# Three experts' weights behind the gather, float64 blocks on ScalarE's queue, routing begun earlier

## The chip, the core and the metric

The kernel runs on one core of a Trainium2 chip. The metric is device time in microseconds (us), the median over several executions. TensorE does the matrix products, VectorE and ScalarE the element work, GpSimd some element work and the indirect DMAs; SyncE issues most other DMAs. Operands live in SBUF, products land in PSUM.

## The reference, cut to what matters

Three stages, each feeding the next.

```python
# attention: q, k, v (2, 8, 768, 64): window of 16 keys beside block summaries
x = attn_out.transpose(0, 2, 1, 3).reshape(1536, 512)
# mixture of 8 experts, each takes 192 tokens, in the order of the gate's logits
logits = x @ w_gate
order = np.argsort(-logits.flatten())
for idx in order:                      # greedy: best logit first
    tok, e = idx // 8, idx % 8
    if assigned[tok] >= 0 or counts[e] >= 192: continue
    assigned[tok] = e; counts[e] += 1
for e in range(8):
    out[assigned == e] = relu(x[assigned == e] @ w1[e]) @ w2[e]
# solu layer: w_in (512, 1024), w_out (1024, 512), both float64
h = x @ w_in
solu = h * softmax(h)
result = (layernorm(solu) * g_ln) @ w_out
```

w_in and w_out are float64 arrays; the kernel loads their two 32-bit words as integers and builds a high and a low float32r part from them.

## The kernel before, in words

**Attention** (to about 103 us) runs over 24 units of four query tiles, with TensorE's and SyncE's order written out by hand in a plan. Its last outputs x are stored to the DRAM tile xd. In it, w_in's first three blocks of float64 are loaded (`load64`, line 58) and split (`split64`, line 63).

**A split** of a block of 128x512 is: ScalarE's Abs with a scale (line 70), three integer steps on VectorE (lines 72, 74, 75), ScalarE's copy to the high part (line 77), and the low part as a difference, on GpSimd in two halves of 256 (line 79). There are 16 blocks, eight of w_in (wiH, wiL) and eight of w_out (woH, woL). Splits carry a priority of -3000, so the planner puts their instructions behind others that are ready; `after` and `late` name an instruction behind which a split is issued.

**Routing.** `route(n)` finds the next expert that fills up and its 192 tokens, without a sort: five levels of a search over the digits of the logits' keys. A level is a comparison on VectorE (`compare`, line 124, tile ge), twelve small products on TensorE (line 502), a step on VectorE (line 507) and one product with ones (lines 510, 516). Then come a chain of small VectorE steps, three products that give positions (lines 548 to 550), two comparisons ohs with their twelve index products each (lines 558 to 563), the index tiles, and `gather`, two indirect DMAs from GpSimd that fetch the token rows xg from xd. As soon as the expert's number is known (line 530), SyncE loads the first three of its eight weight chunks (512 KB each). `route` is a generator: before each of its TensorE steps it yields a time, from the table HOPS, for which TensorE is to be given other work.

**Experts.** Expert n has 32 pieces of four products 128x192 in float32: 16 for w1 (`hidden`, whose result ScalarE copies into hT) and 16 for w2 (`result`, into yh and yl). All eight experts take this path (WHOLE is 7). Products go to one of two PSUM tiles, m1. `tokens(n)` transposes the gathered rows and ScalarE copies them into xs, of which there is one buffer.

**Solu layer.** Tokens leave the experts in tiles of 128, twelve of them. For tile k, `solu_in` is eight pieces of three products 128x512, then the softmax and the norm on VectorE and ScalarE, `solu_t` eight transposes, `solu_out` eight pieces, and an indirect DMA to the output.

**The order of the expert phases.** TensorE's order is the program's. In phase n the 32 pieces of expert n are woven with the solu work of tiles that are ready (`stage2`), and the steps of `route(n + 1)` and `tokens(n + 1)` are put in where the time that they asked for has been filled by pieces. The other engines' orders come from the planner.

**The float64 blocks after the attention.** `todo` lists the 13 blocks left, `steps` the place of each: after a given expert, kind (h or r) and piece group. Two are split with the first routing, the rest in the phases of the first two experts. Loads go through SyncE's queue, three ahead, each waiting for one of three raw buffers.

Of the kernel before, what the change touches and what calls it, by code (L numbers as in the profile page):

```python
# [8 lines left out]
F32 = mybir.dt.float32  # L9
F32R = mybir.dt.float32r  # L10
BF = mybir.dt.bfloat16
I32 = mybir.dt.int32
# [9 lines left out]
def tile_attention_moe_solu(ctx, tc, q, k, v, w_gate, w1, w2, w_in, w_out, g_ln, out):  # L22
# [32 lines left out]
    wiL = keep.tile([128, KD, FF], F32R, name="wiL")  # L55


    def load64(cv, src, n, bufs):
        raw = cv.tile([128, n, 2], I32, name="raw", bufs=bufs)
        dma(raw.rearrange("p n t -> p (n t)"), src.bitcast(I32))  # L60
        return raw

    def split64(cv, raw, hi, lo, after=None, late=None):
        n = hi.shape[1]
        with tc.high_priority(-3000):
            y = cv.tile([128, n], F32, name="cy")
            h = cv.tile([128, n], I32, name="ch", bufs=2)

            with tc.issue_after(after.ins) if after is not None else nullcontext():
                nc.scalar.activation(y, raw[:, :, 1].bitcast(F32), AF.Abs, scale=2.0 ** -112)  # L70
            with tc.issue_after(late.ins) if late is not None else nullcontext():
                nc.vector.tensor_scalar(h, y.bitcast(I32), 3, 0x3FFFFFF8, op0=OP.logical_shift_left,
                                        op1=OP.bitwise_and)
            nc.vector.scalar_tensor_tensor(h, raw[:, :, 1], -0x40000000, h, op0=OP.bitwise_and, op1=OP.bitwise_or)
            nc.vector.scalar_tensor_tensor(h, raw[:, :, 0], 29, h, op0=OP.logical_shift_right, op1=OP.bitwise_or)
            h = h.bitcast(F32)
            nc.scalar.copy(hi, h)
            for c in range(0, n, 256):
                nc.gpsimd.tensor_tensor(lo[:, c:c + 256], h[:, c:c + 256], hi[:, c:c + 256].bitcast(F32), op=OP.subtract)


    ones = keep.tile([128, 128], BF, name="ones")
# [38 lines left out]
    def compare(out, x, a, b, op):  # L121

        n = x.shape[1]
        nc.vector.tensor_tensor(out, x.rearrange("p (j t) -> p j t", t=2)[:, :, None, :].to_broadcast(  # L124
            [128, n // 2, b - a, 2]), ios[:, None, a:b, :].to_broadcast([128, n // 2, b - a, 2]), op=op)
# [305 lines left out]
    NCA = 3  # L431
    RAW64 = {}

    def load_in(cv, i, bufs):
        kk, hf = divmod(i, 2)
        RAW64[i] = load64(cv, w_in[128 * kk:128 * kk + 128, 512 * hf:512 * hf + 512], 512, bufs)

    def split_in(cv, i, *after):
        kk, hf = divmod(i, 2)
# [8 lines left out]
    with tc.manual_schedule(engines={mybir.EngineType.PE, mybir.EngineType.SP}):  # L448
# [3 lines left out]
        for u in sorted(plan):  # L452
# [8 lines left out]
    pm = ctx.enter_context(tc.tile_pool(name="pm", bufs=1, space=PSUM))  # L461


    HOPS = [(1600, 1760, 560, 2200, 2320, 5600),
            (1750, 1540, 490, 2450, 2030, 6300),
            (2620, 2200, 700, 4000, 2900, 8520),
            (2500, 2200, 700, 4500, 2900, 9000),
            (2500, 2200, 700, 2900, 2900, 27000)]
# [4 lines left out]
    def route(ph):  # L473
# [84 lines left out]

        for i, (lo, hi) in enumerate(((0, 128), (128, CAP))):
            compare(ohs[:, :, lo:hi], slot, lo, hi, OP.is_equal)  # L560
            for j in range(NJ):
                nc.tensor.matmul(pi[:, 2 * i:2 * i + 2], ohs[:, j // 2, hi - 128:hi, j % 2], info[:, j, :],
                                 start=j == 0, stop=j == NJ - 1)
# [16 lines left out]
            LI = index(oidx[t0 + 1], 0, 128, 64)  # L580
            IDX[ph] = [(oidx[t0], 128), (oidx[t0 + 1], 64)]
        gather(ph)
        if ph == 0:

            e2 = rp.tile([1, 1], I32, name="e2")
            with tc.issue_after(GI[-1].ins):
                nc.gpsimd.tensor_copy(e2, ei[0:1])
            EREG[ph] = nc.sync.value_load(e2, min_val=0, max_val=E - 1)
            load_w(ph, 3, NCK)
        elif ph <= WHOLE:  # L590
            load_w(ph, 3, NCK)
# [64 lines left out]
    def tokens(ph):  # L656

        o = 0
        if ph > WHOLE:
            xs = mp.tile([128, KD, 2, CAP], F32R, name="xs")  # L660
        else:
            xs = mp.tile([128, 2 * KD, CAP], F32, name="xs")[:, :KD]
        for x, n in XG.pop(ph):
            p = pm.tile([128, 4, 128], F32, name="tr", bufs=2)
            for d in range(KD):
                nc.tensor.transpose(p[:, d, 0:n], x[0:n, 128 * d:128 * d + 128], ident[0:n, 0:n])  # L666
            if ph > WHOLE:
                nc.scalar.copy(xs[:, :, 0, o:o + n], p[:, :, 0:n])
                nc.vector.tensor_tensor(xs[:, :, 1, o:o + n], p[:, :, 0:n], xs[:, :, 0, o:o + n].bitcast(F32),
                                        op=OP.subtract)  # L670
            else:
                nc.scalar.copy(xs[:, :, o:o + n], p[:, :, 0:n])  # L672
            o += n
        XS[ph] = xs
# [27 lines left out]

    def hidden(ph, f, part):
        if f == part == 0:
            HT[ph] = mp.tile([128, KF, 2, CAP], F32R, name="hT") if ph > WHOLE else mp.tile([128, 2 * KF, CAP], F32, name="hT")
        h = HT[ph]
        p = product(ph, W[ph][f // 2], 128 * (f % 2), KD, XS[ph], part)
        if p is None:
            return
        if ph <= WHOLE:  # L710
            after(ph, "h", f, nc.scalar.activation(h[:, f], p[:, :CAP], AF.Relu))  # L711
            return
        s = mp.tile([128, CAP], F32, name="hs", bufs=3)
        nc.scalar.copy(s, p[:, CAP:])
        nc.vector.tensor_tensor(s, s, p[:, :CAP], op=OP.add)
        a = nc.scalar.activation(h[:, f, 0], s, AF.Relu)
        nc.vector.scalar_tensor_tensor(h[:, f, 1], s, 0.0, h[:, f, 0].bitcast(F32), op0=OP.max, op1=OP.subtract)
        after(ph, "h", f, a)
# [103 lines left out]

    nc.vector.memset(mhalf, -0.5)
    ctx.enter_context(tc.manual_schedule(engines={mybir.EngineType.PE}))
    for _ in route(0):
        pass
    dma(gb, g_ln.partition_broadcast(128))
    cvb = tc.tile_pool(name="cvb", bufs=1)
    cvp = cvb.__enter__()

    NRAW = 3
    todo = [(load_in, split_in, i) for i in range(NCA, 2 * KD)]

    def load_out(cv, i, bufs):
        RAW64[8 + i] = load64(cv, w_out[128 * i:128 * i + 128], DM, bufs)

    def split_out(cv, i, after):
        split64(cv, RAW64.pop(8 + i), woH[:, i], woL[:, i], after)

    todo += [(load_out, split_out, i) for i in range(KI)]  # L840
    steps = [None, None, (0, "h", 2), (0, "h", 4), (0, "h", 6), (0, "r", 1), (1, "h", 0), (1, "h", 2), (1, "h", 3),
             (1, "h", 5), (1, "h", 7), (1, "r", 1), (1, "r", 2)]

    def step64(n, *after):
        todo[n][1](cvp, todo[n][2], *after)
        if n + NRAW < len(todo):
            todo[n + NRAW][0](cvp, todo[n + NRAW][2], NRAW)

    for n in range(NRAW):
        todo[n][0](cvp, todo[n][2], NRAW)  # L850
    for n, st in enumerate(steps):
        if st is None:
            step64(n, None, LAST[0])
        else:
            HOOK.setdefault(st, []).append((step64, n))

    p = pm.tile([128, DM], F32, name="o", bufs=1)
    for i in range(40):
        nc.tensor.matmul(p[:, 0:128], ones, tri, start=True, stop=True)
    early = route(1)  # L860
    for _ in range(3):
        next(early)
    tokens(0)
    def weave(a, b):

# [23 lines left out]


    stage2 = ["", "i0", "i1 o0 i2", "o1 i3 o2", "i4 o3 i5", "o4 i6 o5", "i7 o6 i8", "o7 i9 o8", "i10 o9 i11 o10 o11"]
    for ph in range(E):
        u = 540 if ph > WHOLE else 650
        g1 = [(u, hidden, ph, f, i) for f in range(KF) for i in range(KD // 2)]
        g2 = [(u, result, ph, d, i) for d in range(KD) for i in range(KF // 2)]
        other = []
        for k, l in items(stage2[ph]):
            assert k <= last(ph - 1)
            other += l
        if ph == 1:  # L900

            other.append((1300, lambda: None))
        work = weave(g1 + g2, other)

        def ahead(n):
            yield from early if n == 1 else route(n)
            yield HOPS[0 if n <= 1 else 1 if n == 2 else 4 if n == E - 1 else 2 + n % 2][5]
            tokens(n)

        hops = ahead(ph + 1) if ph + 1 < E else iter(())  # L910
        wait = next(hops, None)
        for cost, f, *a in work:
            while wait is not None and wait < cost / 2:
                wait = next(hops, None)
            f(*a)
            if wait is not None:
                wait -= cost
        for _ in hops:
            pass

        if ph == 1:
            cvb.__exit__(None, None, None)
            ml = ctx.enter_context(tc.tile_pool(name="ml", bufs=1))
    for _, l in items(stage2[E]):
        for _, f, *a in l:
            f(*a)
# [30 lines left out]
```

## Time and profile before

| | |
|---|---|
| time, median of 3 runs | 497.45 us (496.35 to 497.51) |
| the profiled execution | 498.66 us |
| its span, first to last instruction | 497.0 us |
| mean granted TensorE clock | 0.968 of full speed |
| TensorE busy | 447.6 us (90%) |
| VectorE busy | 274.3 us (55%) |
| ScalarE busy | 176.0 us (35%) |
| GpSimd busy | 89.0 us (18%) |
| moved by DMA | 64.61 MB, mean 130 GB/s |

Busy times are unions over the span of one execution. PE is TensorE's products, PEld its weight loads, which overlap them; DVE is VectorE, ACT ScalarE, POOL GpSimd, SPq SyncE's queue of DMA issues. The granted clock is the share of full speed that TensorE was given: 1.00 is 2.4 GHz, 0.50 is 1.2 GHz.

### The profile page before, as it was taken

How to read it: one execution, taken by the hardware profiler on the slowest of the kernel's cores; microseconds unless marked ns; L12 is line 12 of the kernel's file. 1: busy time of each engine (PE TensorE's matmuls, PEld its weight loads, DVE VectorE, ACT ScalarE, POOL GpSimd, SP SyncE). 2: the span in 40 equal slices, each digit the busy share in tenths (PEclk: the TensorE clock that was granted, in tenths of full speed). 3: DMA queues.
4: the chain of work that ended last, by engine and by line, in shares of the span. 5: the costliest groups of instructions: out<-in, count | busy, mean ns of one | idle time of the engine just before them, and what ended most of it. 6: DMA issues, size and time to landing. Idle time of an engine off the chain costs nothing.

```text
span 497.0 us, 9767 instructions
## 1 busy us (share of the span) xinstructions
PE 447.6 (90%) x3723; PEld 387.7 (78%) x3723; DVE 274.3 (55%) x1033; ACT 176.0 (35%) x425; POOL 89.0 (18%) x150
## 2 busy tenths in 40 slices
PE   2799999845778988999999999999999999999995
PEld 1668688634678868789888988988898899998773
DVE  7658577878594697675256526626662322213441
ACT  3578778711233432331321413123141313222331
POOL 9311200302324243202000200200020110100012
PEclk9999999975798998999999999999999999999999
DMA  9979861363869159008304800740390560000001
GB/s 195 195 158 207 220 181 40 109 231 131 272 218 368 54 180 316 1 2 279 113 1 137 257 21 1 243 149 1 118 275 30 179 205 1 1 22 1 22 21 42
DMA packets 92463, 64.61 MB, mean 130 GB/s; under 512 B 25728, under 2 KB 87168, under 8 KB 92416
## 3 DMA queue, kind: packets, MB, share of 16 engines
q1 hardware_dynamic: 90432, 57.70, 41.2%
q0 software_dynamic: 1984, 6.29, 3.5%
q8 instruction: 29, 0.48, 0.4%
q14 instruction: 18, 0.15, 0.1%
HBM read 56.51 MB, written 6.29 MB: 126 GB/s over the span
## 4 chain that ended last, share of the span: by engine, by line
PE 71%; DVE 12%; DMA 6%; ACT 5%; issue 3%; SPq 1%; POOL 0%; POOLq 0%; DVEq 0%; ACTq 0%
PE m L694 28%; PE h L759 13%; PE o L802 11%; PE pS L332 4%; PE pO L361 2%; DVE ge L124 2%; DMA xg<-xd,oidx 2%; PE pr L502 2%; PE pA L348 1%; DVE ex L768 1%; DMA wl<-in_moe_w_dram 1%; DMA kn<-in_k_dram 1%; PE tr L666 1%; ACT s L341 1%; PE T L255 1%
## 5 line engine op out<-in xcount | busy, mean ns | idle before, releaser
L694 PE MATMUL m<-xs,wr 128*128 128x192 f32 x384 | 79.7, 341 | 1.2 <-ACT xs L672 1.1
L694 PEld LDWEIGHTS m<-xs,wr 128*128 128x128 f32 x384 | 65.2, 195 | 6.2 <-ACT xs L672 1.4
L742 DVE TENSOR_TENSOR yl<-m,yh 128x128 fp32r<-128x128 f32 (+1 forms) x64 | 16.2, 253 | 82.1 <-ACT yh L741 82.1
L711 ACT ACTIVATE hT<-m 128x192 f32<-128x192 f32 x64 | 21.2, 331 | 90.0 <-PE m L694 76.6
L694 PE MATMUL m<-hT,wh 128*128 128x192 f32 x256 | 51.7, 332 | 0.0
L694 PE MATMUL m<-hT,wl 128*128 128x192 f32 x256 | 50.7, 335 | 0.0
L694 PEld LDWEIGHTS m<-hT,wl 128*128 128x128 f32 x256 | 45.0, 195 | 3.3
L694 PEld LDWEIGHTS m<-hT,wh 128*128 128x128 f32 x256 | 44.5, 193 | 3.7
L741 ACT CAST yh<-m 128x128 fp32r<-128x128 f32 (+1 forms) x64 | 15.2, 238 | 88.9 <-PE m L694 80.6
L341 ACT ACTIVATE s<-s,mx 128x120 f32<-128x120 f32 x96 | 31.5, 387 | 13.6 <-DVE mx L338 13.4
L759 PE MATMUL h<-wiH,yh 128*128 128x512 f32 x96 | 34.4, 446 | 0.0
L332 PE MATMUL pS<-kTw,qbd 128*128 128x120 f32 x192 | 27.8, 290 | 5.8 <-DVE kTw L315 4.8
L777 POOL TENSOR_TENSOR st<-st,mhalf 128x1 f32<-128x1 f32 x12 | 6.9, 574 | 144.8 <-DVE st L776 104.8
L759 PE MATMUL h<-wiL,yh 128*128 128x512 f32 x96 | 32.3, 424 | 0.0
L759 PE MATMUL h<-wiH,yl 128*128 128x512 f32 x96 | 32.2, 424 | 0.0
L802 PE MATMUL o<-woH,lh 128*128 128x512 f32 x96 | 30.8, 432 | 1.3 <-ACT lh L791 1.3
L802 PE MATMUL o<-woL,lh 128*128 128x512 f32 x96 | 32.0, 429 | 0.0
L332 PEld LDWEIGHTS pS<-kTw,qbd 128*128 128x128 f32 x192 | 24.8, 202 | 7.6 <-issue 6.0
L124 DVE TENSOR_TENSOR ge<-e,ios 128x1536 bf16<-128x1536 bf16 (+3 forms) x37 | 29.7, 803 | 0.8
L802 PE MATMUL o<-woH,ll 128*128 128x512 f32 x96 | 29.4, 418 | 0.0
L764 DVE TENSOR_REDUCE st<-h 128x1 f32<-128x1024 f32 x12 | 14.7, 1224 | 26.4 <-PE h L759 26.4
L338 DVE CUSTOM_DVE_ANT_0 s<-pS,mask 128x120 f32<-128x120 f32 x96 | 21.4, 278 | 12.4 <-PE pS L332 5.5
(184 smaller groups left out, 823.5 us busy)
## 6 DMA issues: line engine op xcount, KB each, us to landing
wr<-in_moe_w_dram SPq DMA_DIRECT2D x24, 512.0 KB
wl<-in_moe_w_dram SPq DMA_DIRECT2D x20, 512.0 KB
wh<-in_moe_w_dram SPq DMA_DIRECT2D x20, 512.0 KB
raw<-in_moe_w_in_dram SPq DMA_DIRECT2D x8, 512.0 KB
raw<-in_moe_w_out_dram SPq DMA_DIRECT2D x8, 512.0 KB
Vw<-in_v_dram SPq DMA_DIRECT2D x20, 192.0 KB
kn<-in_k_dram SPq DMA_DIRECT2D x8, 384.0 KB
qn<-in_q_dram SPq DMA_DIRECT2D x8, 384.0 KB
```

Of the source, the lines that this page charges most:

```text
L124: nc.vector.tensor_tensor(out, x.rearrange("p (j t) -> p j t", t=2)[:, :, None, :].to_broadcast([128, n // 2, b - a, 2]), ios[:, None, a:b ...
L332: nc.tensor.matmul(p[:, n, :], qbd[i][:, t, :], kTw[i][:, t, :], start=True, stop=True)
L338: nc.vector.tensor_tensor_reduce(s[:, n, :], p[:, n, :], m, scale=1.0, scalar=3.0e38, op0=OP.add, op1=OP.min, accum_out=mx[:, n:n + 1])
L341: EXPS[u] = nc.scalar.activation(s[:, n, :], s[:, n, :], AF.Exp, bias=mx[:, n:n + 1], scale=-1.0)
L361: nc.tensor.matmul(p[o:o + 64, n // 2, h, :], a[:, n, 64 * h:64 * h + 64], Vw[:, b, t, 2 * hp + h, :], start=True, stop=True)
L694: nc.tensor.matmul(p[:, :CAP], w[:, d, o:o + 128], rhs[:, d], start=d == 0, stop=d == n - 1)
L711: after(ph, "h", f, nc.scalar.activation(h[:, f], p[:, :CAP], AF.Relu))
L741: a = nc.scalar.copy(hi, s[:, s0:s0 + n])
L742: nc.vector.tensor_tensor(YL[k][:, d, c:c + n], s[:, s0:s0 + n], hi.bitcast(F32), op=OP.subtract)
L759: nc.tensor.matmul(ps, a[:, d, :], w[:, d, 512 * s:512 * s + 512], start=n == 0, stop=n == len(mm) - 1)
L764: nc.vector.tensor_reduce(st[:, 0:1], p, axis=AX.X, op=OP.max)
L802: nc.tensor.matmul(p, a[:, f, :], w[:, f, :], start=n == 0, stop=n == len(mm) - 1)
```

## The change

- `load64` can be issued by another engine; the loads of all blocks after the attention but the first two come from ScalarE's queue, the load of block n + 2 at the place of block n's split, ahead of it.
- The low part in `split64` is one subtraction of 512 on VectorE. This holds for all 16 blocks, those in the attention too.
- The blocks' places: five blocks of w_in in the first expert's phase, in the order 4, 6, 3, 5, 7; w_out's eight in the second's (six) and the third's (two). None is split with the first routing any more.
- For the first three routings, not only the first, chunks 3 to 7 of the expert's weights are loaded after the expert's number has been copied by GpSimd behind the gather.
- HOPS: longer times for the first three routings. From the second on there is a yield of 650 between the two ohs comparisons' index products.
- Filler products of 128x128 in bf16, results unused: 18 in each of the last two waits of the first routing, and 90 between the first seven steps of the second routing, which now all stand ahead of the first tokens; before, three steps did, behind 40 fillers.
- The generator of the routings runs on over the phases: after the second expert's tokens, up to five steps of the third routing are put into the first phase.
- xs and hT are half as large (the other half was unused), and the pools cvb and ml are open side by side.

```diff
-    def load64(cv, src, n, bufs):
+    def load64(cv, src, n, bufs, eng=None):
         raw = cv.tile([128, n, 2], I32, name="raw", bufs=bufs)
-        dma(raw.rearrange("p n t -> p (n t)"), src.bitcast(I32))
+        (eng or nc.sync).dma_start(raw.rearrange("p n t -> p (n t)"), src.bitcast(I32))
...
             nc.scalar.copy(hi, h)
-            for c in range(0, n, 256):
-                nc.gpsimd.tensor_tensor(lo[:, c:c + 256], h[:, c:c + 256], hi[:, c:c + 256].bitcast(F32), op=OP.subtract)
+            nc.vector.tensor_tensor(lo, h, hi.bitcast(F32), op=OP.subtract)
...
-    HOPS = [(1600, 1760, 560, 2200, 2320, 5600),
-            (1750, 1540, 490, 2450, 2030, 6300),
+    HOPS = [(1900, 1760, 560, 2300, 2600, 6300),
+            (1900, 1760, 560, 2600, 2600, 7000),
...
             compare(ohs[:, :, lo:hi], slot, lo, hi, OP.is_equal)
+            if i and ph:
+                yield 650
...
-        if ph == 0:
+        if ph < 3:
 
             e2 = rp.tile([1, 1], I32, name="e2")
...
-            xs = mp.tile([128, 2 * KD, CAP], F32, name="xs")[:, :KD]
+            xs = mp.tile([128, KD, CAP], F32, name="xs")
...
-    for _ in route(0):
-        pass
+    idle = pm.tile([128, DM], F32, name="o", bufs=1)
+
+    def fill(n):
+        for _ in range(n):
+            nc.tensor.matmul(idle[:, 0:128], ones, tri, start=True, stop=True)
+
+    for wait in route(0):
+        fill(18 if wait > 2000 else 0)
...
-    todo = [(load_in, split_in, i) for i in range(NCA, 2 * KD)]
+    todo = [(load_in, split_in, i) for i in (4, 6, 3, 5, 7)]
...
-    steps = [None, None, (0, "h", 2), (0, "h", 4), (0, "h", 6), (0, "r", 1), (1, "h", 0), (1, "h", 2), (1, "h", 3),
-             (1, "h", 5), (1, "h", 7), (1, "r", 1), (1, "r", 2)]
+    steps = [(0, "h", 1), (0, "h", 3), (0, "h", 5), (0, "r", 1), (0, "r", 2), (1, "h", 1), (1, "h", 4), (1, "h", 6),
+             (1, "r", 1), (1, "r", 2), (1, "r", 3), (2, "h", 0), (2, "h", 1)]
 
     def step64(n, *after):
+        if n + NRAW - 1 < len(todo):
+            todo[n + NRAW - 1][0](cvp, todo[n + NRAW - 1][2], NRAW, nc.scalar)
         todo[n][1](cvp, todo[n][2], *after)
-        if n + NRAW < len(todo):
-            todo[n + NRAW][0](cvp, todo[n + NRAW][2], NRAW)
...
-    p = pm.tile([128, DM], F32, name="o", bufs=1)
-    for i in range(40):
-        nc.tensor.matmul(p[:, 0:128], ones, tri, start=True, stop=True)
     early = route(1)
-    for _ in range(3):
+    for n in (12, 6, 20, 6, 20, 6, 20):
         next(early)
+        fill(n)
     tokens(0)
...
+    READY = set()
+
+    def ahead():
+        for n in range(1, E):
+            yield from early if n == 1 else route(n)
+            yield HOPS[0 if n <= 1 else 1 if n == 2 else 4 if n == E - 1 else 2 + n % 2][5]
+            tokens(n)
+            READY.add(n)
+            yield 0
+
+    hops = ahead()
+    wait, extra = next(hops), 5
...
             while wait is not None and wait < cost / 2:
+                if ph + 1 in READY:
+                    if ph or extra == 0:
+                        wait = None
+                        break
+                    extra -= 1
                 wait = next(hops, None)
```

## Rows read from the trace of the kernel before

**Rows 1.** Stretches: length; PE, PEld, DVE, ACT, POOL busy; clock, DMA share, GB/s.
```profile
128.80:162.70 33.90, 29.26 (x204) 27.23 (x205) 19.68 (x70) 9.52 (x24) 8.71 (x10) 0.87 0.91 299
162.70:201.80 39.10, 34.21 (x254) 29.73 (x253) 31.20 (x92) 15.30 (x36) 13.20 (x14) 0.96 0.54 172
201.80:476.60 274.80, 272.73 (x1789) 240.77 (x1790) 121.26 (x426) 71.80 (x179) 27.68 (x33) 1.00 0.30 94
```

**Rows 2.** TensorE in order of time: start, duration, line, count, idle before.
```profile
118.55 0.95 PE L562 MATMUL pr<-info,ohs 128*128 128x2 bf16 x24 [1.94 <-DVE ohs L124]
119.36 4.43 PE L859 MATMUL o<-tri,ones 128*128 128x128 bf16 x40
...
127.66 0.69 PE L666 MATMUL tr<-ident,xg 64*128 64x64 f32 x4 [0.18 <-DMA xg<-xd,oidx]
...
148.10 6.10 PE L694 MATMUL m<-hT,wl 128*128 128x192 f32 x36
...
156.60 0.66 PE L666 MATMUL tr<-ident,xg 128*128 128x128 f32 x4 [0.83 <-DMA xg<-xd,oidx]
157.09 5.75 PE L694 MATMUL m<-hT,wl 128*128 128x192 f32 x24
```

**Rows 3.** TensorE's waits, first and second phase: total us, times, longest.
```profile
PE tr L666 <- DMA xg<-xd,ix: 1.1, 1, 1.1
...
PE tr L666 <- DMA xg<-xd,oidx: 0.8, 1, 0.8
...
PE m L694 <- ACT xs L672: 1.1, 1, 1.1
```

**Rows 4.** TensorE by microsecond: length, busy, then clock, DMA share, GB/s.
```profile
106.00:107.00 1.00, 0.00 (x0) 0.80 0.72 238
...
133.00:134.00 1.00, 1.00 (x15) 0.55 1.15 348
```

**Rows 5.** VectorE in order of time.
```profile
106.11 0.96 DVE L124 TENSOR_TENSOR ge<-e,ios 128x1536 bf16<-128x1536 bf16 x1
106.99 0.16 DVE L506 SCALAR_TENSOR_TENSOR eb<-e,d5b 128x12 f32<-128x12 bf16 x1
...
108.28 0.96 DVE L124 TENSOR_TENSOR ge<-e,ios 128x1536 bf16<-128x1536 bf16 x1
...
117.54 1.43 DVE L124 TENSOR_TENSOR ohs<-slot,ios 128x1536 bf16<-128x1536 bf16 x2
...
125.70 2.89 DVE L506 SCALAR_TENSOR_TENSOR eb<-e,d5b 128x12 f32<-128x12 bf16 x1
...
141.05 0.71 DVE L525 TENSOR_SCALAR ine<-r,r 128x12 f32<-128x12 f32 x1
...
145.27 2.46 DVE L124 TENSOR_TENSOR ohs<-slot,ios 128x1536 bf16<-128x1536 bf16 x2
...
188.05 0.78 DVE L606 SCALAR_TENSOR_TENSOR wt<-slot,wt 128x96 f32<-128x96 bf16 x1
```

**Rows 6.** GpSimd in order of time.
```profile
120.74 3.57 POOL L649 DMA_INDIRECT xg<-xd,oidx  x1 [22.24 <-DVE ch L72]
...
125.80 2.76 POOL L79 TENSOR_TENSOR wiL<-ch,wiH 128x256 fp32r<-128x256 f32 x4
...
145.14 2.17 POOL L79 TENSOR_TENSOR wiL<-ch,wiH 128x256 fp32r<-128x256 f32 x2 [3.41 <-ACT wiH L77]
...
150.30 1.37 POOL L649 DMA_INDIRECT xg<-xd,oidx  x1 [0.30 <-PE m L694]
```

**Rows 7.** Instructions by line: VectorE's last integer step of a split; busy, mean.
```profile
L75 DVE SCALAR_TENSOR_TENSOR ch<-raw,ch 128x512 int32<-128x512 int32 x16 | 11.1, 696 | 0.1
```

**Rows 8.** Stretch late in the attention, VectorE alone: length, busy, clock, DMA share.
```profile
86.00:92.80 6.80, 6.72 (x33) 1.00 0.24 81
```

**Rows 9.** SyncE's queue in order of time.
```profile
155.34 25.86 SPq L60 DMA_DIRECT2D raw<-in_moe_w_out_dram  x6
```

**Rows 10.** Instructions that touch the raw tile: shortest, median, longest in ns.
```profile
L60 SPq DMA_DIRECT2D raw<-in_moe_w_out_dram x8: 327/328/3186, 139.7 to 180.9; - x8
```

More of the change, by code (lines that the diff above doesn't have):

```diff
@@ L432, in tile_attention_moe_solu, with load_in @@
     RAW64 = {}
-    def load_in(cv, i, bufs):
+    def load_in(cv, i, bufs, eng=None):
         kk, hf = divmod(i, 2)
-        RAW64[i] = load64(cv, w_in[128 * kk:128 * kk + 128, 512 * hf:512 * hf + 512], 512, bufs)
+        RAW64[i] = load64(cv, w_in[128 * kk:128 * kk + 128, 512 * hf:512 * hf + 512], 512, bufs, eng)
     def split_in(cv, i, *after):
@@ L704, in hidden @@
         if f == part == 0:
-            HT[ph] = mp.tile([128, KF, 2, CAP], F32R, name="hT") if ph > WHOLE else mp.tile([128, 2 * KF, CAP], F32, name="hT")
+            HT[ph] = mp.tile([128, KF, 2, CAP], F32R, name="hT") if ph > WHOLE else mp.tile([128, KF, CAP], F32, name="hT")
         h = HT[ph]
@@ L824, in tile_attention_moe_solu, with load_out @@
     ctx.enter_context(tc.manual_schedule(engines={mybir.EngineType.PE}))
-    for _ in route(0):
-        pass
+    idle = pm.tile([128, DM], F32, name="o", bufs=1)
[4 more added lines that the diff above has]
+        fill(18 if wait > 2000 else 0)
     dma(gb, g_ln.partition_broadcast(128))
-    cvb = tc.tile_pool(name="cvb", bufs=1)
-    cvp = cvb.__enter__()
+    cvp = ctx.enter_context(tc.tile_pool(name="cvb", bufs=1))
+    ml = ctx.enter_context(tc.tile_pool(name="ml", bufs=1))
     NRAW = 3
-    todo = [(load_in, split_in, i) for i in range(NCA, 2 * KD)]
-    def load_out(cv, i, bufs):
-        RAW64[8 + i] = load64(cv, w_out[128 * i:128 * i + 128], DM, bufs)
+    todo = [(load_in, split_in, i) for i in (4, 6, 3, 5, 7)]
+    def load_out(cv, i, bufs, eng=None):
+        RAW64[8 + i] = load64(cv, w_out[128 * i:128 * i + 128], DM, bufs, eng)
     def split_out(cv, i, after):
@@ L840, in tile_attention_moe_solu @@
     todo += [(load_out, split_out, i) for i in range(KI)]
-    steps = [None, None, (0, "h", 2), (0, "h", 4), (0, "h", 6), (0, "r", 1), (1, "h", 0), (1, "h", 2), (1, "h", 3),
-             (1, "h", 5), (1, "h", 7), (1, "r", 1), (1, "r", 2)]
+    steps = [(0, "h", 1), (0, "h", 3), (0, "h", 5), (0, "r", 1), (0, "r", 2), (1, "h", 1), (1, "h", 4), (1, "h", 6),
+             (1, "r", 1), (1, "r", 2), (1, "r", 3), (2, "h", 0), (2, "h", 1)]
     def step64(n, *after):
+        if n + NRAW - 1 < len(todo):
+            todo[n + NRAW - 1][0](cvp, todo[n + NRAW - 1][2], NRAW, nc.scalar)
         todo[n][1](cvp, todo[n][2], *after)
-        if n + NRAW < len(todo):
-            todo[n + NRAW][0](cvp, todo[n + NRAW][2], NRAW)
-    for n in range(NRAW):
+    for n in range(NRAW - 1):
         todo[n][0](cvp, todo[n][2], NRAW)
     for n, st in enumerate(steps):
[L852 to L855, printed above, removed]
-    p = pm.tile([128, DM], F32, name="o", bufs=1)
-    for i in range(40):
-        nc.tensor.matmul(p[:, 0:128], ones, tri, start=True, stop=True)
+        HOOK.setdefault(st, []).append((step64, n))
     early = route(1)
-    for _ in range(3):
+    for n in (12, 6, 20, 6, 20, 6, 20):
         next(early)
+        fill(n)
     tokens(0)
@@ L903, in tile_attention_moe_solu @@
         work = weave(g1 + g2, other)
[L905 to L911, printed above, removed]
         for cost, f, *a in work:
             while wait is not None and wait < cost / 2:
+                if ph + 1 in READY:
[3 more added lines that the diff above has]
+                    extra -= 1
                 wait = next(hops, None)
@@ L917, in tile_attention_moe_solu @@
                 wait -= cost
[L918 to L923, printed above, removed]
+        while ph + 1 < E and ph + 1 not in READY:
+            wait = next(hops)
+        if wait is None or ph:
+            wait = next(hops, None)
     for _, l in items(stage2[E]):
```

## The prediction

> **What bounds the kernel now.** I read the busy shares by stretch first, cut where the kernel changes its kind of work: the first expert's phase (128.8 to 162.7 us), the second's (to 201.8), and all that follows up to the end of the last solu input products [rows 1]. The reader is to see that the page's 90% for TensorE is a mean over unlike stages. From 201.8 to 476.6 TensorE is busy 272.73 of 274.80 us at the full granted clock: only less TensorE work could shorten that. The first two phases are different: 29.26 of 33.90 us and 34.21 of 39.10 us busy, with a mean granted clock of 0.87 and 0.96. So a change that leaves the products alone can earn something only before 201.8, and whatever it earns there moves the end by as much. What is lost there: idle 4.64 + 4.89 = 9.5 us; and a mean of 0.87 between levels of 1.2 and 2.4 GHz means 26% of the stretch at the lower one, where half the time is lost, 0.13 x 33.9 + 0.04 x 39.1 = 6.0 us. Together 15.5.
>
> Next TensorE's instructions in order of time [rows 2]: the 36 products from 148.10 took 6.10 us, 0.169 each, so a piece of four is 0.68 and an expert's 32 pieces 21.7; the 24 from 157.09 took 5.75, 0.24 each, so 1.7 us were lost there, right behind the wait for the gathered tokens (the transposes at 156.60). Of the waits in the two phases, the tokens' DMA accounts for 1.9 us and ScalarE's copies of them for 1.1 [rows 3]; I put the other 6.5 us of idle time down to VectorE's routing steps, which TensorE waits for in between. The clock fell at 106 us, in the first routing, where TensorE has hardly any work, and it was low again until 133.9, five microseconds into the first expert [rows 4].
>
> Last, VectorE and GpSimd, which hold each other up [rows 5, 6]. The tiny step L506 took 0.16 us at 106.99 and 2.89 at 125.70, where it ended just after GpSimd's four low-part subtractions (125.80 for 2.76). The two ohs comparisons took 1.43 us at 117.54 and 2.46 at 145.27, under GpSimd's 145.14 to 147.31. The other way round, GpSimd's first gather took 3.57 us at 120.74, while VectorE worked through two weight splits, the one at 150.30 1.37.
>
> **The change, part by part.** *Low parts to VectorE.* GpSimd loses two subtractions per block; VectorE gains one of 128x512 fp32. The nearest row is L75, also two inputs from SBUF of that size: a mean of 0.696 [rows 7], 0.61 from one to the next. I take 0.61, bounds 0.4 (as if half of it were hidden) and 0.7. Eleven blocks fall in the two phases: +6.7 us of VectorE's time. Against that goes the stretching: ten instructions in the two phases, from L525 at 141.05 to L606 at 188.05, about 0.5 us too long each, 5.4 us in all [rows 5]. The Trainium skill, "SBUF — State Buffer", section Who interferes with whom, says that a VectorE instruction with two SBUF inputs and a GpSimd instruction that reads SBUF shut each other out for the whole of one of them. The rows agree (2.89 against 0.16 us); by that rule all of the 5.4 come back, by the rows shown at least the 2.0 of three of them.
>
> In the attention three of these subtractions join VectorE, which there is busy 6.72 of 6.80 us [rows 8]. I take +0.6 us on the path, one of the three; bounds 0 (all find a gap) and 1.9 (none does).
>
> *Second expert's routing taken further ahead.* Two splits no longer stand between the first index step and the gather, and seven steps of that routing instead of three precede the first tokens in TensorE's order. One level takes 2.17 us (comparison to comparison, 106.11 and 108.28) [rows 5]. From about 120.7 the third level's products end some 5 us later, at 125.7; with the last 20 fillers the first transposes come at about 127, and the second set of transposes started at 127.66 before [rows 2]. So the first expert starts where it did: 0, bounds -0.5 and +2 (the fillers at half clock: 90 at 0.11 us, from 40 in 4.43, are 10 us instead of 5, of which the comparisons' waits hide half or more). Its phase sheds two levels of twelve small products, 24 of which take 0.95 [rows 2]: -0.9.
>
> *Fillers.* 18 stand in each of the first routing's last two waits, 2.0 us at 0.11, where the second wait was 1.94 [rows 2]: +0.2 in all. TensorE then works closely from about 114.5 on, where it began the 40 at 119.4. I take it that the clock has risen before the first expert starts and finds no gap to fall in: -6.0, bounds 3 (it rises as late as before) and 6.
>
> *Third routing begun in the first phase, longer pauses, one more pause between the two ohs comparisons.* Counted out from the code, the second expert's tokens stand behind piece 24 of 32 instead of 26, two levels of the third routing follow in the same phase, and the third expert's tokens stand behind piece 32 of the next phase's 40, not 36. The pauses grow from 1600 and 2200 to 1900 and 2300 to 2600, some 0.3 us of slack each: about half a VectorE instruction, so it removes some waits and not all.
>
> *Weights behind the gather.* For three experts chunks 3 to 7 now leave after the gather. Its tokens came 4.9 us after the issue's end at 151.67 (150.30 + 1.37), while DMA moved 299 GB/s over the phase [rows 1, 6]; the first gather's were all there 3.4 us after its issue ended. So a gather gets at least 1.5 us faster, and the pause in front of the tokens grows from 5600 to 6300: the 1.9 of token waits and the 1.1 of copies go. The cost is that 2.6 MB leave later, 8.8 us at 299 GB/s; the gather stands behind piece 14 of 32, and the fourth chunk is first used twelve pieces into the next phase: 30 pieces or 20 us later. Hidden.
>
> *Blocks from ScalarE's queue, over three phases.* SyncE stood from 155.34 for 25.86 us at six of these loads [rows 9], so weights queued behind them; that ends. An issue takes 0.33 us [rows 10]; eleven on ScalarE, with room, are hidden unless they wait (below). The Trainium skill, "DMA: Bandwidth & Descriptors", section Issuing engines are not separate DMA queues, holds that issuing from another engine saves only issue time. No run here shows it yet; by it this edit is worth 0, which is also what I enter.
>
> **Sum.** VectorE's work in the two phases was 19.68 + 31.20 = 50.9 us. Two levels leave (a comparison of 0.96 and three small steps, 1.35 each: -2.7), the low parts come (+6.7), the stretching goes (-5.4), the splits are as many: 49.5. Without any loss the phases would take 73.0 - 15.5 - 0.9 = 56.6, so VectorE would be busy 87% of it, in a fixed order: not every wait goes. Of the 6.5 us of idle that I put down to it I let half go, for want of a better row. So: clock -6.0, tokens and copies -3.0, VectorE's waits -3.25, levels -0.9, attention +0.6, fillers +0.2: -12.35. The profiled execution took 498.66 us, its span 497.0 and 1.66 around it, and stands 1.2 above the median of 497.45: 486.3 in its own time, 485.1 beside the median.
>
> **The rivals.** (a) *VectorE becomes the bound.* All 6.7 us of low parts stand on the path: 491.8. For it: 87% load and in-order issue, so a split ahead of a routing step costs up to 0.7. Against: splits carry the lowest priority, and w_out's may slip into the third phase, where all of VectorE's 121.26 us have 274.80 of room [rows 1].
>
> (b) *The gathers starve.* VectorE's denser two-input work stretches an issue to 3.57 us as it did the first [rows 6], or both of an expert's: 2.6 to 5.2 late. The pause holds ten pieces, 6.8 us; two issues at 1 and 3.4 to land need 5.4; so 1.2 to 3.8 of idle in each phase, say 2, and 1.7 of half clock behind it: 485.1 + 7.4 = 492.5. [...] Against: the issue of 1.37, beside a split.
>
> (c) *Slower: ScalarE waits.* The load of block n+2 takes the buffer of block n-1 and now stands among the copies that empty TensorE's products. Hooks are as close as four pieces, 2.7 us, and the second product buffer covers two pieces more, 1.4. Where a split lags more than 4.1 us behind its hook, TensorE stops, at up to eleven places. It decides at a mean lag of 4.1 + 12.35/11 = 5.2 us. SyncE's six loads came at 4.3 us each in just this wait [rows 9]. At a lag of 5.6: 485.1 + 16.5 = 501.6.
>
> (d) *No change.* The fourth chunk comes so late that what is gained is given back at the phase's end: 496 to 499. It needs 12 us more than I count.
>
> **How the numbers follow.** Forecast 0.60 (480 to 489.5), (a) 0.16, (b) 0.10, (c) 0.10, (d) 0.04. A measurement here tells about 0.3%, 1.5 us. The low end is all 15.5, 0.9 and the 2.1 us idle of the long stage recovered, less half a microsecond for the attention: 479.5. The high end takes in (a) and (b): 492.5. Faster 0.86, same 0.04, slower 0.10.
>
> **What would show it.** Right: a granted clock near 1 from 120 us on; phases near 29 and 33 us; no subtraction on GpSimd and L506 near 0.16 throughout; a long stage of the same 275 us. Wrong: the first expert starting after 131, clock dips in front of the tokens, ScalarE's copies waiting behind loads, or a longer third phase.

## The result and the profile after

The changed kernel took 482.57 us (median of four executions, 481.84 to 484.21), the kernel before 497.48 beside it: a ratio of 0.9708, 95% interval 0.9678 to 0.9738. It is faster by 14.9 us; forecast were 12.35. The profiled execution took 481.84, its span 480.1. The same three stretches as in [rows 1], by busy time:

```profile
126.40:153.60 27.20, 25.07 (x202) 23.34 (x203) 19.63 (x73) 10.04 (x25) 2.06 (x3) 1.00 0.90 278
153.60:184.05 30.45, 30.34 (x229) 27.65 (x227) 25.16 (x85) 12.62 (x31) 3.04 (x3) 1.00 0.73 233
184.05:459.40 275.35, 272.99 (x1789) 240.29 (x1788) 128.62 (x440) 75.89 (x187) 26.31 (x31) 1.00 0.31 99
```

The first expert's phase went from 33.9 to 27.2 us, the second's from 39.1 to 30.45; together they are 15.35 shorter, and the long stage is as long as it was (+0.55). From the first routing's first product to the first expert's start it is 25.30 us before and 25.23 after; six of the variants below that share this stretch (five that take a part back, all but the one without fillers, and the doubled low parts) need 25.9 to 26.2, so up to a microsecond of it is this execution's luck. In five of those six the clock fell once more among the fillers, for 3.4 us, and in the sixth it first rose at 122.3 us; here it stayed up. One microsecond of the variant that begins the third routing later:

```profile
120.00:121.00 1.00, 1.00 (x11) 0.50 1.00 345
```

The profiled executions lie 16.8 apart, 1.5 more than the phases say, since the attention ended 2.3 sooner (the first routing's first product at 101.19 us instead of 103.51), and the stages behind the phases gave 0.85 back. Of the 2.3, 1.2 are there at the first scores, which began at 12.76 us instead of 13.96 behind a k load that landed sooner; that is no part of the change. So the phases are the result.

In them the granted clock is 1.00 and 1.00, where it was 0.87 and 0.96. TensorE's idle time fell from 9.5 us to 2.13 + 0.11. Its waits in the first phase (total us, times, longest); the second has none:

```profile
PE pr L563 <- DVE ohs L123: 1.3, 1, 1.3
PE tr L667 <- DMA xg<-xd,oidx: 0.4, 1, 0.4
PE pr L547 <- DVE row L539: 0.4, 1, 0.4
PE m L695 <- ACT xs L673: 0.2, 1, 0.2
```

Tokens and copies had cost 3.0 us [rows 3]; 0.6 is left. TensorE in order of time:

```profile
112.00 2.08 PE L831 MATMUL o<-tri,ones 128*128 128x128 bf16 x18
...
114.09 1.46 PE L831 MATMUL o<-tri,ones 128*128 128x128 bf16 x18
...
124.86 0.99 PE L667 MATMUL tr<-ident,xg 128*128 128x128 f32 x8
125.79 0.46 PE L501 MATMUL pr<-oh,ge 128*128 128x8 bf16 x12
126.42 0.43 PE L695 MATMUL m<-xs,wr 128*128 128x192 f32 x1 [0.17 <-ACT xs L673]
...
146.66 0.66 PE L667 MATMUL tr<-ident,xg 128*128 128x128 f32 x4 [0.44 <-DMA xg<-xd,oidx]
```

The reader is to see two things. The fillers run from 112 us, seven microseconds earlier than the 40 of [rows 2], or five when both are counted from the first routing's first product. And the first expert's eight transposes carry no bracket: the tokens were there, TensorE's own order of work came to them late. Three microseconds of the clock show what the fillers did, and what a short wait did not:

```profile
114.00:115.00 1.00, 1.00 (x16) 0.63 0.00 0
115.00:116.00 1.00, 0.55 (x10) 1.00 0.27 73
137.00:138.00 1.00, 0.27 (x11) 1.00 0.96 291
```

It rose in the 115th microsecond, amid the second 18 fillers, and stayed, also over the 1.30 us wait for ohs that ends at 137.73.

GpSimd in order of time, to set against [rows 6]: its first gather takes 1.18 us instead of 3.57, and no subtraction is left between the gathers.

```profile
118.32 1.18 POOL L650 DMA_INDIRECT xg<-xd,oidx  x1 [42.94 <-DVE ge L123]
119.81 0.91 POOL L650 DMA_INDIRECT xg<-xd,oidx  x1 [0.31 <-DVE e L511]
...
140.68 0.93 POOL L650 DMA_INDIRECT xg<-xd,ix  x1 [19.75 <-DVE oidx L570]
141.92 0.95 POOL L650 DMA_INDIRECT xg<-xd,oidx  x1 [0.30 <-issue]
```

VectorE, against [rows 5]: the step that took 2.89 us takes 0.16, a low part 0.68, and the ohs comparisons 1.42 for two instead of 2.46. What TensorE waited for at 137.73 stands ahead of them: a split, in VectorE's order in front of the comparison.

```profile
125.00 0.16 DVE L505 SCALAR_TENSOR_TENSOR eb<-e,d5b 128x12 f32<-128x12 bf16 x1
...
133.72 0.68 DVE L78 TENSOR_TENSOR wiL<-ch,wiH 128x512 fp32r<-128x512 f32 x1
...
135.30 0.68 DVE L74 SCALAR_TENSOR_TENSOR ch<-raw,ch 128x512 int32<-128x512 int32 x1
...
136.13 0.68 DVE L75 SCALAR_TENSOR_TENSOR ch<-raw,ch 128x512 int32<-128x512 int32 x1
136.73 1.42 DVE L123 TENSOR_TENSOR ohs<-slot,ios 128x1536 bf16<-128x1536 bf16 x2
```

Where the clock was low before is worth a second look, for the sum hangs on it. Of the kernel before, TensorE's ohs waits in the second phase, and the clock by microsecond:

```profile
187.18 0.45 PE L562 MATMUL pr<-info,ohs 128*128 128x2 bf16 x12 [1.34 <-DVE ohs L124]
188.18 0.45 PE L562 MATMUL pr<-info,ohs 128*128 128x2 bf16 x12 [0.55 <-DVE ohs L124]
```

```profile
157.00:158.00 1.00, 1.00 (x8) 0.90 1.15 348
158.00:159.00 1.00, 1.00 (x5) 0.50 1.20 376
...
188.00:189.00 1.00, 0.82 (x14) 0.76 1.11 393
190.00:191.00 1.00, 1.00 (x4) 0.50 1.13 352
```

There were three low stretches, not one. The first reached from the first expert's start at 128.81 to 133.9 [rows 4] and cost half of that, 2.5 us. The second, 3.4 us of low clock and so 1.7 lost, stands right behind the two token waits of 1.12 and 0.83. The third, also 3.4 us, stands right behind the two ohs waits above, 1.34 and 0.55. So 2.5 of the 6.0 us belong to the start, the rest to waits in the phases: each of those pairs cost its 1.9 us of idle time and then almost as much again at 1.2 GHz.

### The profile page after: what moved, and what is told of

It is laid out like the page before. It is cut to its first block, busy times and chain, and to the rows that moved or that the text cites. A ratio compares the mean times of both kernels' runs of the same rounds, so it can differ in the third digit from the quotient of the medians.

```text
span 480.1 us, 9909 instructions
## 1 busy us (share of the span) xinstructions
PE 444.0 (92%) x3809; PEld 385.4 (80%) x3809; DVE 273.8 (57%) x1049; ACT 175.1 (36%) x425; POOL 58.9 (12%) x120
## 4 chain that ended last, share of the span: by engine, by line
PE 74%; DVE 13%; ACT 4%; DMA 4%; issue 3%; POOL 1%; POOLq 0%; SPq 0%; ACTq 0%; DVEq 0%
PE m L695 30%; PE h L760 13%; PE o L803 11%; PE pS L331 4%; PE pO L360 2%; DVE ge L123 2%; PE pr L501 2%; PE pA L347 2%; PE tr L667 1%; DVE ex L769 1%; PE T L291 1%; PE T L254 1%; PE T L299 1%; DMA kn<-in_k_dram 1%; DVE ch L74 1%
## 5 line engine op out<-in xcount | busy, mean ns | idle before, releaser
L695 PE MATMUL m<-xs,wr 128*128 128x192 f32 x384 | 77.4, 333 | 0.2 <-ACT xs L673 0.2
L695 PEld LDWEIGHTS m<-xs,wr 128*128 128x128 f32 x384 | 63.2, 190 | 4.7 <-PE o L803 0.8
L695 PE MATMUL m<-hT,wh 128*128 128x192 f32 x256 | 49.9, 327 | 0.0
L695 PE MATMUL m<-hT,wl 128*128 128x192 f32 x256 | 49.2, 327 | 0.0
L695 PEld LDWEIGHTS m<-hT,wl 128*128 128x128 f32 x256 | 43.3, 189 | 3.2
L695 PEld LDWEIGHTS m<-hT,wh 128*128 128x128 f32 x256 | 43.3, 189 | 3.2
L501 PEld LDWEIGHTS <-ge 128*128 128x128 bf16 (+1 forms) x420 | 13.8, 96 | 15.2 <-DVE ge L123 10.2
```

Source lines behind the costliest of these rows:

```text
L501: nc.tensor.matmul(pr[0:nb, 0:E], ge[:, j // 2, :nb, j % 2], oh[:, j, :], start=j == 0, stop=j == NJ - 1)
L695: nc.tensor.matmul(p[:, :CAP], w[:, d, o:o + 128], rhs[:, d], start=d == 0, stop=d == n - 1)
```

## The experiments

First six kernels that take one part of the change back; their medians stand beside 482.57, their ratios beside 0.9708.

**Only the first expert's weights behind the gather.**

```diff
-        if ph < 3:
+        if ph == 0:
```

> The changed kernel with chunks 3 to 7 behind the gather for the first expert only, as before the change. Theory that weights in flight slow the gather: the tokens of the second and third expert land about 5 us after the issue's end instead of 3.7, TensorE waits 1 to 2 us in front of each set of transposes, and the time rises by 1.5 to 4 us, the upper end if the clock falls in those waits. Rival, that the longer pause in front of the tokens hides it: 0 to 0.7 us.

491.77 us, ratio 0.9872 (0.9823 to 0.992): 9.2 us slower, far more than expected. The phases were 31.29 and 34.15 us. TensorE in order of time, then the clock:

```profile
148.81 0.46 PE L667 MATMUL tr<-ident,xg 64*128 64x64 f32 x4 [1.44 <-DMA xg<-xd,ix]
150.65 1.12 PE L667 MATMUL tr<-ident,xg 128*128 128x128 f32 x4 [1.39 <-DMA xg<-xd,oidx]
```

```profile
150.00:151.00 1.00, 0.35 (x2) 0.77 1.11 337
151.00:152.00 1.00, 1.00 (x6) 0.50 1.15 348
```

The gather's second issue ended at 144.41, so its tokens came 6.2 us later; in the changed kernel they came 3.8 us after 142.87. Both tiles were waited for, 2.8 us in all, and then the clock was low for 3.4 us, which cost another 1.7. The second phase had 1.8 us more of token waits, and 1.4 of idle time at its end whose releaser the profile does not show. The theory had the direction and the place; it left out that a token wait is paid for twice.

**Low parts back on GpSimd.**

```diff
-            nc.vector.tensor_tensor(lo, h, hi.bitcast(F32), op=OP.subtract)
+            for c in range(0, n, 256):
+                nc.gpsimd.tensor_tensor(lo[:, c:c + 256], h[:, c:c + 256], hi[:, c:c + 256].bitcast(F32), op=OP.subtract)
```

> The changed kernel with the low parts of all splits back on GpSimd, in two halves. Theory that GpSimd and VectorE shut each other out: VectorE loses 16 subtractions of 0.6 us but its small steps are stretched again, about 0.5 us for each pair it meets, and gathers queue behind low parts; TensorE's waits in the first two phases go from about 2 us to 4 to 7, and the time rises by 2 to 5 us. Rival, that VectorE has room either way and the move is neutral: within 1 us of the changed kernel.

486.82 us, ratio 0.979 (0.9745 to 0.9835): 4.2 slower, inside the theory's range, but not at its place: TensorE's waits in the two phases came to 3.0 us, not 4 to 7. The phases give 0.95 of the difference of the profiled executions, and what follows them 1.75, where w_out's subtractions now meet VectorE's steps; the other 1.7 lie ahead of the first expert, where most of the variants stand behind the change's profiled execution by as much. GpSimd in order of time, and TensorE's waits behind the phases:

```profile
195.00 4.42 POOL L79 TENSOR_TENSOR woL<-ch,woH 128x256 fp32r<-128x256 f32 x4 [1.36 <-ACT woH L77]
```

```profile
PE pr L510 <- DVE sat L507: 1.7, 3, 1.0
```

Four of these took 2.76 us where little stood against them [rows 6]. The Trainium skill, "SBUF — State Buffer", section Who interferes with whom, has the two engines lock each other out in just this pairing; 4.42 here, and 0.16 for VectorE's step in the changed kernel without it, agree. The first gather says nothing of it: with the low parts back on GpSimd its issue took 1.18 us, as in the changed kernel.

```profile
119.44 1.18 POOL L651 DMA_INDIRECT xg<-xd,oidx  x1 [22.27 <-DVE ge L124]
```

**No fillers.**

```diff
-        for _ in range(n):
+        for _ in range(0):
```

> The changed kernel without any filler product, everything else in its order. Theory that fillers bring only the rise of the clock ahead of the first expert: the first expert's phase starts about 1 us earlier, since the last 20 fillers are gone, and at half clock for 3 to 5 us, which loses half of that; the later dips stay away, since the gaps that caused them are gone: 0.5 to 2.5 us slower. Rival, that all 6 us of half clock of the kernel before come back: 5 us slower.

484.21 us, ratio 0.9736 (0.9688 to 0.9784): 1.6 slower by the medians, with intervals that overlap, so it is the phases that decide. The first was 29.07 us, 1.8 longer, the second 30.39 as before; the first expert started 24.42 us behind the routing's first product, 0.8 sooner without fillers to work off. TensorE by microsecond:

```profile
129.00:130.00 1.00, 1.00 (x5) 0.50 1.15 348
130.00:131.00 1.00, 1.00 (x10) 0.98 1.15 346
```

The first expert's own products brought the clock back by 130. The fillers save half of 126.28 to 130.02, 1.9 us, and cost 0.8, or 1.7 against the six variants named above: a microsecond at most by the profiles, 1.6 by the medians. The rival, by which the whole 6 us hang on them, fell either way.

**No step of the third routing in the first phase.**

```diff
-    wait, extra = next(hops), 5
+    wait, extra = next(hops), 0
```

> The changed kernel with no step of the third routing in the first expert's phase. Theory that its early start only takes VectorE's work out of the second phase: there TensorE has no wait now, and the third tokens go to the phase's very end: 0.5 to 2 us slower. Rival, that it carries the second phase's whole gain: 4 us or more slower.

485.5 us, ratio 0.977 (0.972 to 0.982): 2.9 slower by the medians. The phases were 26.17 and 32.12 us: what the first phase is spared, 1.1, the second pays with 1.7. That is 0.7 in all, and 0.3 more comes after them. The profiled execution, the fastest of its four, lies 2.5 above that of the change; the other 1.6 stand ahead of the first expert, 0.7 in the attention and 0.9 between the first routing and the first expert, as in the other variants, and are not this edit's. The three executions without a profile took 1 to 2 us more, at a mean granted clock of 0.974 to 0.978 against 0.981; no trace shows where. The intervals of this kernel and the changed one overlap. The theory's 0.5 to 2 us hold for what the profile shows; the rival fell.

**The pauses of the kernel before.**

```diff
-    HOPS = [(1900, 1760, 560, 2300, 2600, 6300),
-            (1900, 1760, 560, 2600, 2600, 7000),
+    HOPS = [(1600, 1760, 560, 2200, 2320, 5600),
+            (1750, 1540, 490, 2450, 2030, 6300),
```

> The changed kernel with the pauses in front of the second and third experts' routing steps set back to those of the kernel before (1600, 1760, 560, 2200, 2320, 5600 and 1750, 1540, 490, 2450, 2030, 6300); all else as changed. The kernel before with both the low parts on VectorE and the weights behind the gather came to 488.6 us, about 6 above the changed kernel, and the fillers measured 1.6 of that, the third routing's early start 2.9. Theory: the longer pauses are worth most of what is left, since a routing step is then asked for after VectorE has it ready, and tokens after they have come: 485 to 488 us, with waits of 1.5 us or more in the two phases. Rival: the further-ahead routing alone gives the slack, and the pauses do nothing: 482 to 484 us, phases of 27 to 28 and 30 to 31.

484.99 us, ratio 0.9773 (0.9729 to 0.9817), 2.4 slower, with intervals that just overlap: by the time the theory's low end. The phases, 27.99 and 30.99, are those that the rival named, 1.3 us longer in sum than the change's. One wait of TensorE's is back:

```profile
PE tr L667 <- DMA xg<-xd,oidx: 1.7, 1, 1.7
```

The clock did not fall behind it. So in the phases the pauses are worth about the wait for the second expert's tokens, and nothing beyond; the rest of the 2.4 us is not in them.

**Block loads on SyncE.**

```diff
-            todo[n + NRAW - 1][0](cvp, todo[n + NRAW - 1][2], NRAW, nc.scalar)
+            todo[n + NRAW - 1][0](cvp, todo[n + NRAW - 1][2], NRAW)
```

> The changed kernel with all block loads back in SyncE's queue, at the same places and two ahead. Theory that only issue time is saved: within 1 us. Rival, that SyncE's in-order waits for VectorE's buffers hold weights up (and that its waits for experts' numbers hold blocks up): 2 to 6 us slower, with TensorE waiting for weights or for the second expert's solu products.

483.53 us, ratio 0.9706 (0.9661 to 0.975): no difference by the ratio; phases of 27.0 and 30.53. Its median stands 0.96 above the change's all the same, although its phases are as short, so about a microsecond of each of these differences of medians need not be the edit's. The "DMA: Bandwidth & Descriptors" page of the Trainium skill, section Issuing engines are not separate DMA queues, allows the other queue nothing but issue time, and this run agrees. Nor does ScalarE's queue cost anything, as its instructions at this line of the changed kernel show (shortest, median, longest in ns):

```profile
L60 ACTq EVENT_SEMAPHORE  x13: 17/38/2658, 101.2 to 181.7; - x13
L60 ACTq DMA_DIRECT2D raw<-in_moe_w_out_dram x8: 334/334/335, 141.9 to 186.9; - x8
```

The longest of thirteen waits was 2.66 us, below the 4.1 from which rival (c) would have begun to cost.

Then three kernels that make one or two parts alone in the kernel before, against 496.3 to 496.5 us beside them.

**Low parts on VectorE alone**, the edit above the other way round.

> The kernel before with the low parts on VectorE and nothing else changed. Theory that GpSimd and VectorE shut each other out: the first gather is no longer stretched by a 3.57 us issue, and the stretched steps fall back to their own length; half of what undoing it cost the changed kernel and the earlier first gather together make it 3 to 5 us faster. Rival, that the waits of the kernel before are those for tokens and clock, which it leaves: within 1.5 us.

492.73 us, ratio 0.9921 (0.9894 to 0.9948): 3.9 faster, as expected, but not by the first of the reasons. The first gather's issue took as long as before:

```profile
119.02 3.57 POOL L648 DMA_INDIRECT xg<-xd,oidx  x1 [42.93 <-DVE ch L72]
```

The first expert started 25.28 us behind the first routing's first product, as before (25.30). With both parts, below, this issue took 3.58 us. These kernels still split two blocks with the first routing, and the changed kernel does not: that ended the long issue, not the low parts' move. What the move brought lies in the phases, 33.28 and 35.58 us: the second lost 3.5, and no low clock is left in it. **Three experts' weights behind the gather alone:**

```diff
-        if ph == 0:
+        if ph < 3:
```

> The kernel before with chunks 3 to 7 behind the gather for the first three experts and nothing else changed. Theory that the weights in flight are what holds the tokens up: undoing it cost the changed kernel 9 us, so 5 to 9 us faster, with the clock's dips at 158 and 189 gone. Rival, that SyncE's queue, which still carries the float64 blocks, then holds the weights up: 0 to 3 us faster, with TensorE or SyncE waiting there.

491.07 us, ratio 0.9872 (0.9821 to 0.9922): 6.4 faster, with phases of 30.31 and 37.53 us. The two show each other's half. TensorE's token wait with the low parts alone:

```profile
154.33 0.95 PE L665 MATMUL tr<-ident,xg 128*128 128x128 f32 x4 [1.81 <-DMA xg<-xd,oidx]
```

The clock fell at 154.6, right behind that wait. And with the weights alone, no token wait over 0.4 is left, but the pair of ohs waits stands as before, GpSimd's subtractions beside it, and the clock falls in the second of them, at 183.6:

```profile
182.78 0.45 PE L562 MATMUL pr<-info,ohs 128*128 128x2 bf16 x12 [1.36 <-DVE ohs L124]
183.78 0.48 PE L562 MATMUL pr<-info,ohs 128*128 128x2 bf16 x12 [0.55 <-DVE ohs L124]
```

```profile
183.00:184.00 1.00, 0.45 (x18) 0.80 0.95 314
186.00:187.00 1.00, 1.00 (x4) 0.50 0.00 0
```

**Both.**

> The kernel before with the two parts together that were tried alone: low parts on VectorE and three experts' weights behind the gather. Theory that the two act on different waits and add: 3.9 and 6.4 us make 9 to 11 us faster, and what is left of the change's 15 us, some 4 to 6, is the fillers and the order of routing and splits. Rival, that both shorten the same wait for tokens: no better than 7 us.

488.59 us, ratio 0.9844 (0.9808 to 0.9879): 7.7 faster, below the theory's 9 to 11, which the interval (6.0 to 9.5) just reaches; the sum of the two is 10.3, so they overlap in part. In the phases its clock was low only at the first expert's start, until 132.1, as the kernel before had it to 133.9. So these two edits carry half of the gain. Its phases are 6.8 us longer than the change's, and 2.5 of that is the low clock. The other half lies with the rest of the change: the fillers, the pauses and the third routing, which taken back one by one are worth 1.6, 2.4 and 2.9 us by the medians, and the blocks' new places and order, which no run takes back alone. How it divides among them is not shown.

**Every low part computed twice**, to see how much room VectorE has.

```diff
             nc.vector.tensor_tensor(lo, h, hi.bitcast(F32), op=OP.subtract)
+            nc.vector.tensor_tensor(lo, h, hi.bitcast(F32), op=OP.subtract)
```

> The changed kernel with every low part computed twice on VectorE: 16 more subtractions of 0.6 us, 11 of them in the first two phases, two in the third. Theory that VectorE has room, as its waits in the changed kernel say: 0 to 2.5 us slower. Rival, that VectorE is close to being the bound: 5 to 8 us slower.

490.13 us, ratio 0.9846 (0.9789 to 0.9902): 7.6 slower. My theory that VectorE has the room fell, for the attention and the first phase. Three low parts more in the attention put off the first routing's first product to 105.38 us, 3.0 to 3.5 us later than in the six kernels that take a part back; those in the first phase made one wait longer, and the clock did the rest (TensorE in order of time, then by microsecond):

```profile
143.84 0.48 PE L564 MATMUL pr<-info,ohs 128*128 128x2 bf16 x12 [2.23 <-DVE ohs L124]
```

```profile
143.00:144.00 1.00, 0.16 (x6) 0.81 1.06 362
144.00:145.00 1.00, 1.00 (x15) 0.50 1.07 365
```

This is the 1.30 us wait of the changed kernel, 0.9 longer. It stayed low until 150.4, 3.4 us lost: the first phase took 30.63 us, 3.4 longer. The second took 30.81, only 0.4 longer with six more subtractions: there VectorE had the room.

Last, two variants of the changed kernel. **The second routing taken three steps ahead instead of seven:**

```diff
-    for n in (12, 6, 20, 6, 20, 6, 20):
+    for n in (12, 6, 20):
```

> The changed kernel with three steps of the second routing ahead of the first tokens, as before, and 38 fillers between them instead of 90. Theory that those levels are worth their place: two levels go back into the first expert's phase, where VectorE is at its edge, and the second expert's tokens to its end: 1 to 4 us slower, although the first expert can start 1 to 2 us earlier. Rival, that they only hold the first tokens up: 0 to 2 us faster.

484.09 us, ratio 0.9744 (0.9696 to 0.9791): not to be told from the changed kernel. The first expert starts 2.2 us earlier behind the routing (23.03), and the phases take 2.8 more (28.22 and 32.21): moved, not saved. With 52 fillers fewer the clock was low from 125.0 to 128.5 us, at the first expert's start, and 1.7 of the 2.8 are that. **Longer pauses for the second expert's tokens, and other fillers:**

```diff
-    HOPS = [(1900, 1760, 560, 2300, 2600, 6300),
+    HOPS = [(1900, 1760, 560, 2300, 3900, 6950),
...
-    for n in (12, 6, 20, 6, 20, 6, 20):
+    for n in (20, 6, 24, 6, 20, 6, 0):
```

> The changed kernel with the first expert's pauses in front of the ohs index products and of the tokens longer by two pieces and one (3900 and 6950), with 20, 6, 24, 6, 20, 6 and 0 fillers, which closes the 0.55 and 0.31 us in which TensorE waits between the fillers and lets the first tokens' transposes go 1.1 us earlier. Theory: the 1.3 us wait for ohs and the 0.4 us for tokens go, the first expert starts 1 us earlier and finds the clock up more often: 1.5 to 3.5 us faster than the changed kernel. Rival, that the tokens come no earlier and the third routing, two pieces later, gives the rest back: within 1 us.

480.83 us (six executions), ratio 0.9686 (0.966 to 0.9711): 1.7 below the changed kernel, at the low end of what was expected, and the intervals overlap. Its phases, 25.25 and 32.05 us, are 0.3 shorter in sum. Whether it is faster stays open.

## Why the prediction was right, and which terms were not

**The place** was right: all of the gain lies in the two phases (forecast near 29 and 33 us, measured 27.2 and 30.4), the long stage kept its 275 us, and the first expert started where it had.

**The clock, -6.0.** The sum came out: 0.87 and 0.96 became 1.00 and 1.00. The step that failed is the cause: "finds no gap to fall in" stood under the fillers. Without them 1.9 us are lost again, not 6. Some 3.4 of the 6 us hung on the token waits and the ohs waits, and went because those went: the weights alone removed the low clock behind the one, the low parts alone that behind the other. That the sum came out under a cause that holds for a third of it is luck; by the run without fillers, they alone would have earned some 4 us less than entered.

**Tokens and copies, -3.0.** 2.4 us of idle time went, as the profile counts it, but the edit under which I put it is worth 9.2 us taken out of the changed kernel and 6.4 put alone into the kernel before. That is the mis-sized term: to a wait for tokens belongs the low clock behind it.

**VectorE's waits, -3.25 of 6.5.** Some 1.7 us are left (ohs 1.30, row 0.4), so 4.8 went; letting half go was too careful. The stretching of VectorE's instructions by GpSimd was a part of the mechanism: in the kernel before its end took 3.5 us out of the second phase. It was not the whole, since with the low parts back on GpSimd the changed kernel's phases were only 0.95 longer; what the pauses and the blocks' places took of the rest is not shown apart. Beside it, busy time at full clock fell by 2.1 us instead of 0.9.

**Attention, +0.6.** It was 0: low parts back on GpSimd did not bring the first routing forward (102.21 us, the other variants of the change 101.5 to 102.4). The room was small, though: the three doubled subtractions cost 3.0 to 3.5. **ScalarE's queue, 0**, was right, and the 0 for the first expert's start within a microsecond (25.9 to 26.2 in six variants, 25.30 before); the fillers' +0.2 is not shown apart from it.

**The rivals.** (a) did not happen with one low part per block; with two it does in the attention and the first phase, and not in the second. Nine low parts fell into the two phases, not eleven; four slipped into the third, as the rival's own counter-argument had it. (b) did not: the first three experts' gather issues took 0.91 to 1.45 us, 1.18 for the one that took 3.57, since no split stands with the first routing any more. (c) and (d) did not.

The kernels without the third routing's early start and with the low parts on GpSimd cost some 1.5 to 2 us more by their medians than their phases and what follows show; in their profiled executions 1.6 to 1.7 us of it stand ahead of the first expert, as in the other variants, and so are not these edits'. Open is how far that holds for the executions without a profile, and whether the last variant is better than the change.

## What to carry to other kernels

Where TensorE's granted clock dips, look at what stood idle just ahead of each dip, and charge the dip to that wait: two waits of 1.3 and 0.6 us cost 3.6 here, and an edit that removed them was worth about double what the table of waits says. Take parts back one by one as well as putting them in alone; here the single prices (9.2, 4.2, 2.9, 2.4, 1.6) sum to far more than the 14.9 us gained. One reason is that a gap opened by any part brings the low clock with it, as with the weights taken back; another, that about a microsecond of each may not be its own. And test an engine's room by doubling the work you gave it, not by its busy share: in the first phase, 72% busy, four more subtractions of 0.6 us cost 3.4 us, because one stood ahead of the ohs comparison that TensorE waits for and the clock fell in that wait; in the second, 83% busy, six more cost 0.4.

## What the runs showed of the hardware that was not expected

A single wait of 1.30 us (after) or 1.67 us (old pauses) left the clock at 1.00, and so did 0.34 and 0.55 with twelve small products between (before, at 147.8 us). It fell behind 1.12 and 0.83 us with four transposes between (before), 1.34 and 0.55 (before) and 1.36 and 0.55 (weights alone) with twelve small products between, 1.44 and 1.39 (weights taken back), 0.79 and 1.81 (low parts alone), and one of 2.23 (doubled). Each of these dips cost 1.7 us, the one of the doubled low parts 3.4. A gather of 192 tokens landed 6.2 us after its issue's end beside the weights' loads, 3.8 us when they had been held back behind it. And GpSimd's issue of a gather took 3.57 or 3.58 us while VectorE worked through two splits without a pause, wherever their low parts ran, and 1.18 us without them.
